# Attention and routed experts on one core: first expert rows loaded in a row, a router product in another bank, and written orders for TensorE and SyncE

## Chip, cores, metric

One core of a Trainium2 chip. The metric is the device time of one launch in microseconds (us); a change of under about 0.2% can't be told from none.

## What is computed

For each of 8 batches of 1856 rows: attention with squared ReLU, its output times u, and a two-level router (4 groups of 4 experts, the best group, then its best expert) in front of 16 experts of 256 x 1024 x 256. All is float32.

```python
scores = scale * np.matmul(z, z.transpose(0, 2, 1))
attn = np.maximum(scores, 0.0) ** 2
x = (u * np.matmul(attn, v)).reshape(B * S, D)
g_idx = np.argmax(x @ w_group, axis=1)          # g_w: its softmax
e_idx = np.argmax(xg @ w_expert[g], axis=1)     # e_w: its softmax
h = np.maximum(xg[mask_e] @ w1[g, e], 0.0)
out[tok_idx] = (g_w * e_w)[:, None] * (h @ w2[g, e])
```

## The kernel before

**Products in parts.** A float32 operand is split into a rounded high part and the rest, and a product is made of three passes (high by high, high by low, low by high). TensorE (PE) is busy with these nearly all the time.

**Attention** runs in 480 steps: 8 batches, 4 chunks of columns (512, 512, 512, 320), 15 blocks of keys each. `scores` runs some steps ahead of `attn_v`, which adds into the banks `o` (L409) with operands `al`, `ah` that VectorE (DVE) and ScalarE (ACT) make (L360, L361). At the end of a chunk `chunk_end` forms the chunk's rows `xT` (L431), splits them (`xh`, `xl`), and defers by step numbers: the router product `pl` (L486, L487, two pairs of products in a bank of `ps_m`), its copy `lgp` (ACT L494), a transposing load `lgx` on SyncE's queue (SP L497), and the transposed rows `rows` (SP L473).

**Routing.** The generator `route` is a chain of small DVE operations, a few at each step: it starts from `lgx` (L555), goes through the one-hot `oh` (L581) to the running counts `pre` (L602, L605), has two small PE products `pk` (L617 from `oh`, L618 from `pre`), and from these the places `di` (L630). GpSimd (POOL) then scatters the rows into `bucket` in HBM (L653). In the last batch chunks 2 and 3 are routed apart; they are named (7,2) and (7,3) here. The steps behind the last attention step are run by `early`, between the parts of the first two expert blocks.

**Experts 0 to 3** run as 12 blocks of up to 512 columns of the bucket (block 0 is 512 columns, 1: 512, 2: 384, 3: 320, 4: 256, 5: 368, 6: 512, 7: 256, 8: 336, 9: 304, 10: 256, 11: 512). Block i takes `xp_i` (a transposing load on SP, L790) and `meta_i` (L793) by `load_x`, `join_x` (DVE copy `xf`, L804; ACT `xh_m`, L809; DVE `xl_m`, L810), 48 products `ph` (L825 to L827) whose results go through `hh` (ACT L830) and `hl` (DVE L836), and 48 products `yT` (L910), copied to `yp` (ACT L913) and transposed back into `yr` on SP (L923) for the weighted scatter to the output. Blocks 0 and 1 use rows that were sorted earlier; block 2 and all later ones need every row scattered, those of (7,3) too (`more_rows` waits till `deferred` and `gens` are empty). The weights of experts 1 to 3 are loaded (`raw_e`, SP L184, L187) and split (L196, L197, L203, L204) inside an earlier block. Experts 4 to 15 follow with an order written for all engines, and are not touched.

**Order.** Within attention and blocks a scheduler orders each engine's instructions by its own model, except where `tc.manual_schedule` keeps the written order. Before, SP keeps it through the attention's end and blocks 0 and 1 (`queue`, closed at `i == NEARLY`, NEARLY = 2); PE, DVE, ACT and POOL are the scheduler's in all 12 blocks. Each engine and the SP queue run their instructions in their order: a waiting one holds all behind it.

Of the kernel before, what the change touches and what calls it, by code (L numbers as in the profile page):

```python
# [9 lines left out]
F32 = mybir.dt.float32  # L10
# [3 lines left out]
U16 = mybir.dt.uint16  # L14
# [5 lines left out]
P = 128  # L20
# [9 lines left out]
def tile_glu_attn_moe(  # L30
# [16 lines left out]
    ND = D // P  # L47
# [66 lines left out]
    def new_pl(name):  # L114
        return sb("pl", [P, 2048], U16, 2, name)
# [4 lines left out]
    def bank(pl, tag, name):  # L120
        return pl.tile([P, 512], F32, tag=tag, name=name)
# [94 lines left out]
    def new_w():  # L216
        return {"h": [], "l": [], "2": []}
# [203 lines left out]
    def chunk_end(s):  # L421
# [56 lines left out]
        pls = []  # L478

        def logits():  # L480
            ps = bank(ps_m, "m", f"pl_{b}_{c}")
            pls.append(ps)
            xh, xl = xhl
            held = pin if last else same
            for d in range(ND):
                held(nc.tensor.matmul(ps[0:LP, 0:w], whl[:, d, :], xh[:, d, 0:w], start=(d == 0), stop=False))  # L486
                nc.tensor.matmul(ps[0:LP, 0:w], wh0[:, d, :], xl[:, d, 0:w], start=False, stop=(d == ND - 1))  # L487
# [10 lines left out]
                lgx.rearrange("p t h l -> p (t h) l"), lgp[:, 0:nt].rearrange("p t h q -> p (t h q)")  # L498
            )

        LG = (7 if b == B - 1 and c < 2 else (9 if c == 2 else 8 if c == 0 else 7)) if s + 1 < NS - NK else 6 if last else 2
        XO = 2 if s + 1 < NS - NK else 0
        (split_x() if XO == 0 else defer(s + XO, split_x))
        (rest_x() if XO == 0 else defer(s + XO + 1, rest_x))
# [6 lines left out]
        defer(s + LG + (1 if XO else 0), logits_out)  # L511
        if not XO:
            defer(s + (7 if last else 5), to_rows)
        wait = 8 if last else (17 if c == 1 and b < B - 1 else 12 if c == 1 else 15) if s + 1 < NS - NK else 11
        alone = b == B - 1 and c >= NQ - 2
        if c % 2 or alone:
            gens.append((max(s + wait, PFILL[-1] + 2), route(b, c // 2, (c % 2,) if alone else (0, 1))))
# [8 lines left out]
    def run_gens(step, n):  # L526
        while gens and gens[0][0] <= step and n > 0:
            try:
                gap = next(gens[0][1])
                n -= 1  # L530
                if gap and step < 10 ** 9:
                    gens[0] = (step + gap, gens[0][1])
            except StopIteration:
                gens.pop(0)
# [251 lines left out]

    def load_x(name, r0, n):

        xp = new_pl(f"xp_{name}").rearrange("p (g q) -> p g q", g=4)
        nc.sync.dma_start_transpose(xp[:, :, 0:n], bucket16[ds(r0, n), 0:2 * D])  # L790
        meta = sb("meta", [P, 4, 2], I32, 7, f"meta_{name}")
        nt = (n + P - 1) // P
        nc.sync.dma_start(  # L793
            meta[:, 0:nt, :], bucket[ds(r0, nt * P), D:D + 2].rearrange("(t p) w -> p t w", p=P)
        )
        return xp, meta
# [239 lines left out]
    for s in range(NS):  # L1036
# [33 lines left out]
            prep_zm(nxt // NQ, nxt % NQ)  # L1070
        if s == NS - NK:
            load_rows(0)
        if s == NS - 9:
            load_rows(1)
        if s == NS - 8:
            xs.append(join_x(0, rows_b[0][0], blocks[0][2]))
# [16 lines left out]

    def early(i):
        run_deferred(late["at"])
        run_gens(late["at"], 4)
        late["at"] += 1
        more_rows(i)

# [322 lines left out]
    unsent = []  # L1422
    FILL = {1: (0, 1), 2: (2, 3), 7: (4, 5)}
    x = xs[0]
    for i, (e, r0, n) in enumerate(blocks):
        if i == NEARLY:
            queue.close()
        if i == 0:
            ld = 1
        else:  # L1430
            pe_ = blocks[i - 1][0]
            ld = pe_ + 2 if last_use[pe_] == i - 1 and pe_ + 2 < NOLD else None
        sp = []
        if ld is not None:
            wts[ld] = new_w()
            sp = [load_w(regs(ld)[0], wts[ld], pc, f"e{ld}") for pc in range(4)]

        def mid(f):
            if i < NEARLY:
# [27 lines left out]
        more_rows(i)  # L1467
        for j in FILL.get(i, ()):
            fill(j)
        if not last:  # L1470
            x = join_x(i + 1, rows_b[i + 1][0], blocks[i + 1][2])
        if i + 2 == NB:
# [17 lines left out]

        unsent = phase2_t(f"b{i}" if last else i, wts[e], hs, rows_b.pop(i)[1], n, next_view, mid2) or unsent

    duo_banks()
    in_order = ExitStack()
    written.append(True)
# [154 lines left out]
```

## Time and profile before

| | |
|---|---|
| median of 3 runs | 1420.11 us (1420.0 to 1420.81) |
| profiled execution | 1423.28 us, span 1421.5 us |
| TensorE, granted clock | busy 1409.7 us (99% of the span), clock 1.00 |
| DVE, ACT, POOL busy | 86%, 73%, 31% |
| blocks 0 to 11 | from 754 to 956 us of the span |

TensorE is the engine that sets the time, so what counts is where it pauses. A PE row of a timeline gives the start of a product and its modelled duration; products overlap, so the time between two starts is what one costs (about 0.23 us with 512 columns, 0.12 with 256). A pause is a longer step between two starts, and the brackets name what ended it.

### The profile page before, as it was taken

Reading aid. Unit: us, or ns where it says so; the run is one execution under the profiler, and the core shown is the slowest. Engines: PE = TensorE matmul, PEld = TensorE weight load, DVE = VectorE, ACT = ScalarE, POOL = GpSimd, SP = SyncE. Lnnn points to the kernel's source line nnn. Section 1 sums busy time; section 2 is a strip of 40 time slices with the busy share of each in tenths; the row PEclk is TensorE's granted clock in tenths of the full one; section 3 lists DMA queues with packets and bytes.
Section 4 is the critical chain, followed back from the end, with each engine's and each line's share of the span. In section 5 each row is a group of like instructions: output and inputs, shape, how many; then the busy total and the mean of one; then the engine's idle time right before and its main releaser. Section 6 shows DMA issues by size and latency. Waiting matters only on the chain.

```text
span 1421.5 us, 22629 instructions
## 1 busy us (share of the span) xinstructions
PE 1409.7 (99%) x6986; PEld 1216.5 (86%) x6986; DVE 1216.7 (86%) x2433; ACT 1042.2 (73%) x1836; POOL 435.1 (31%) x460
## 2 busy tenths in 40 slices
PE   9999999999999999999999999999999999999998
PEld 7888888888888888888788898988888888899997
DVE  7989999999989989999897578689777788888884
ACT  8877887787877878788775354357777777777773
POOL 0002012220222112201223232332445555555554
PEclk9999999999999999999999999999999999999999
DMA  6978979989899899897986476536565555566652
GB/s 235 250 189 228 243 167 257 237 203 226 188 254 228 191 240 211 225 239 165 244 207 159 126 206 146 118 84 145 141 146 131 147 142 136 141 152 151 154 140 59
DMA packets 402411, 257.78 MB, mean 181 GB/s; under 512 B 243827, under 2 KB 356238, under 8 KB 402288
## 3 DMA queue, kind: packets, MB, share of 16 engines
q1 hardware_dynamic: 390384, 225.29, 66.1%
q0 software_dynamic: 11824, 30.90, 7.9%
q8 instruction: 55, 0.90, 0.3%
q14 instruction: 68, 0.56, 0.1%
q10 hardware_dynamic: 80, 0.13, 0.0%
HBM read 110.65 MB, written 88.33 MB: 140 GB/s over the span
## 4 chain that ended last, share of the span: by engine, by line
PE 85%; DVE 6%; DMA 3%; issue 2%; ACT 2%; POOL 1%; SPq 1%; DVEq 0%; POOLq 0%; ACTq 0%
PE o L409 35%; PE duo_p L910 15%; PE duo_y L1372 6%; PE yT L910 4%; PE sc L371 4%; PE sc L372 4%; PE ph L825 2%; PE ph L826 2%; PE ph L827 2%; PE duo_w L1372 2%; PE duo_x L1372 2%; PE duo_p L1372 2%; PE duo_z L1372 2%; DMA out_dram<-y_w,meta_w 1%; PE pl L487 1%
## 5 line engine op out<-in xcount | busy, mean ns | idle before, releaser
L409 PE MATMUL o<-ah,vl 128*128 128x512 f32 (+1 forms) x960 | 354.5, 370 | 0.4 <-DVE ah L383 0.4
L409 PE MATMUL o<-ah,vh 128*128 128x512 f32 (+1 forms) x960 | 354.2, 369 | 0.0
L409 PE MATMUL o<-al,vh 128*128 128x512 f32 (+1 forms) x896 | 328.8, 369 | 0.2 <-DVE al L361 0.2
L653 POOL DMA_INDIRECT bucket<-rows,di x120 | 133.8, 1115 | 379.2 <-issue 220.1
L375 ACT ACTIVATE r<-sc 128x512 f32<-128x512 f32 (+1 forms) x300 | 172.5, 575 | 70.2 <-PE sc L372 49.8
L409 PEld LDWEIGHTS o<-ah,vl 128*128 128x128 f32 x960 | 180.2, 188 | 31.8 <-DVE ah L383 1.1
L409 PEld LDWEIGHTS o<-ah,vh 128*128 128x128 f32 x960 | 180.2, 188 | 30.0
L954 POOL DMA_INDIRECT out_dram<-y_w,meta_w x92 | 138.5, 1506 | 192.6 <-ACT y_w L948 145.3
L386 DVE TENSOR_TENSOR al<-r,ah 128x512 fp32r<-128x512 f32 (+1 forms) x268 | 181.0, 676 | 15.4 <-DVE ah L383 0.5
L409 PEld LDWEIGHTS o<-al,vh 128*128 128x128 f32 x896 | 167.9, 188 | 27.6 <-DVE al L386 0.4
L910 PE MATMUL duo_p<-hh_w,duo_w 128*128 128x496 f32 (+10 forms) x692 | 177.7, 371 | 0.0
L382 ACT ACTIVATE r<-r 128x512 f32<-128x512 f32 (+1 forms) x266 | 163.8, 616 | 8.5
L910 PEld LDWEIGHTS duo_p<-hh_w,duo_w 128*128 128x128 f32 x692 | 128.6, 188 | 16.7
L383 DVE CAST ah<-r 128x512 fp32r<-128x512 f32 (+1 forms) x266 | 109.8, 413 | 24.0 <-ACT r L382 20.3
L371 PE MATMUL sc<-zm,z2h 128*128 128x512 f32 (+1 forms) x300 | 116.6, 389 | 0.5 <-DVE zm L273 0.4
L372 PE MATMUL sc<-zm,z2l 128*128 128x512 f32 (+1 forms) x300 | 115.1, 384 | 0.0
L311 DVE STREAM_TRANSPOSE mt<-r 128x512 f32<-128x512 f32 x157 | 110.7, 705 | 0.7
L910 PE MATMUL duo_p<-hl_w,duo_w 128*128 128x496 f32 (+10 forms) x346 | 104.1, 371 | 0.0
L361 DVE TENSOR_TENSOR al<-at,ah 128x512 fp32r<-128x512 f32 (+1 forms) x180 | 101.3, 577 | 2.0 <-ACT ah L360 1.9
L360 ACT CAST ah<-at 128x512 fp32r<-128x512 f32 (+1 forms) x180 | 91.7, 530 | 7.6 <-DMA sym<-mt 5.0
L910 PE MATMUL yT<-hh,w_e 128*128 128x512 f32 (+6 forms) x352 | 74.1, 328 | 0.0
L954 POOL DMA_INDIRECT out_dram<-y,meta x33 | 39.6, 1199 | 106.4 <-DVE y L953 78.9
(263 smaller groups left out, 2879.6 us busy)
## 6 DMA issues: line engine op xcount, KB each, us to landing
sym<-mt SPq DMA_DIRECT2D x134, 256.0 KB
duo_r<-in_w_dram SPq DMA_DIRECT2D x48, 512.0 KB
at<-sym SPq DMA_DIRECT2D x88, 256.0 KB
bucket<-padrow SPq DMA_DIRECT2D x28, 528.0 KB
at<-sym SPq DMA_DIRECT2D x92, 160.0 KB
ut<-in_uT_dram SPq DMA_DIRECT2D x24, 512.0 KB
vr<-in_v_dram SPq DMA_DIRECT2D x23, 512.0 KB
raw_e<-in_w_dram SPq DMA_DIRECT2D x16, 512.0 KB
```

The costliest lines, as they stand in the source:

```text
L311: nc.vector.transpose(out=t2.rearrange("p (j t x) -> p t j x", t=KT, x=32), in_=a.rearrange("p (t j x) -> p t j x", t=KT, x=32))
L371: held(nc.tensor.matmul(ps[:, 0:w], z2h[:, ks], zm, start=True, stop=False))
L372: held(nc.tensor.matmul(ps[:, 0:w], z2l[:, ks], zm, start=False, stop=True))
L375: held(nc.scalar.activation(out=a, in_=ps[:, 0:w], func=AF.Relu, scale=1.0 / S))
L382: held(nc.scalar.activation(out=a, in_=a, func=AF.Square))
L383: held(nc.vector.tensor_copy(out=ah, in_=a))
L386: held(nc.vector.tensor_sub(out=al, in0=a, in1=f32(ah)))
L409: held(nc.tensor.matmul(oa[d][:, 0:QW[b][c]], (vh if q else vl)[:, d0:d0 + P], al if q == 2 else ah, start=(i == 0 and q == 0), stop=end a ...
L653: nc.gpsimd.indirect_dma_start(out=views[(b * NQ + 2 * half + hs[h]) * NT + i], out_offset=bass.IndirectOffsetOnAxis(ap=di[0:n, i0 + i:i0 ...
L910: nc.tensor.matmul(o, wt["2"][f // 2][:, w0:w0 + P], hs[f][q // 2][:, c0:c0 + n], start=(at == 0), stop=(at == 3 * NF - 1))
L954: nc.gpsimd.indirect_dma_start(out=outs(), out_offset=bass.IndirectOffsetOnAxis(ap=meta[0:m, t, 1:2], axis=0), in_=y[0:m], in_offset=None, ...
L1372: nc.tensor.matmul(out, a, b, start=(q == 0 and m in (1, 5)), stop=(q == 2), skip_group_check=True)
```

## The change

1. `load_x`: the rows of block 0 (`xp_0`) go into a buffer of the tag `ut` (2 buffers) rather than of the tag of `new_pl`; and `load_rows(1)` runs 5 steps earlier, one step behind `load_rows(0)`.
2. The last router product, that of (7,3), goes into a bank of `ps_s` (used by scores and `ph`) rather than of `ps_m`, one step earlier (LG 5 for 6); its routing starts one step earlier (wait 7 for 8), and each `early` runs 5 steps of a generator for 4.
3. PE runs blocks 0 and 1 in the written order too (`region`).
4. SP keeps the written order through all 12 blocks (`queue.close()` stands behind the loop), and the next expert's weights are asked for one block earlier (`needs`, `ask`, `asked`).

```diff
--- before.py
+++ after.py
@@ -478,7 +478,7 @@
         pls = []
 
         def logits():
-            ps = bank(ps_m, "m", f"pl_{b}_{c}")
+            ps = bank(*((ps_s, "s") if last else (ps_m, "m")), f"pl_{b}_{c}")
             pls.append(ps)
             xh, xl = xhl
             held = pin if last else same
@@ -498,7 +498,7 @@
                 lgx.rearrange("p t h l -> p (t h) l"), lgp[:, 0:nt].rearrange("p t h q -> p (t h q)")
             )
 
-        LG = (7 if b == B - 1 and c < 2 else (9 if c == 2 else 8 if c == 0 else 7)) if s + 1 < NS - NK else 6 if last else 2
+        LG = (7 if b == B - 1 and c < 2 else (9 if c == 2 else 8 if c == 0 else 7)) if s + 1 < NS - NK else 5 if last else 2
         XO = 2 if s + 1 < NS - NK else 0
         (split_x() if XO == 0 else defer(s + XO, split_x))
         (rest_x() if XO == 0 else defer(s + XO + 1, rest_x))
@@ -511,7 +511,7 @@
         defer(s + LG + (1 if XO else 0), logits_out)
         if not XO:
             defer(s + (7 if last else 5), to_rows)
-        wait = 8 if last else (17 if c == 1 and b < B - 1 else 12 if c == 1 else 15) if s + 1 < NS - NK else 11
+        wait = 7 if last else (17 if c == 1 and b < B - 1 else 12 if c == 1 else 15) if s + 1 < NS - NK else 11
         alone = b == B - 1 and c >= NQ - 2
         if c % 2 or alone:
             gens.append((max(s + wait, PFILL[-1] + 2), route(b, c // 2, (c % 2,) if alone else (0, 1))))
@@ -786,7 +786,11 @@
 
     def load_x(name, r0, n):
 
-        xp = new_pl(f"xp_{name}").rearrange("p (g q) -> p g q", g=4)
+        if name == 0:
+            xp = sb("ut", [P, ND, 512], F32, 2, f"xp_{name}").rearrange("p c q -> p (c q)").bitcast(U16)
+        else:
+            xp = new_pl(f"xp_{name}")
+        xp = xp.rearrange("p (g q) -> p g q", g=4)
         nc.sync.dma_start_transpose(xp[:, :, 0:n], bucket16[ds(r0, n), 0:2 * D])
         meta = sb("meta", [P, 4, 2], I32, 7, f"meta_{name}")
         nt = (n + P - 1) // P
@@ -1070,7 +1074,7 @@
             prep_zm(nxt // NQ, nxt % NQ)
         if s == NS - NK:
             load_rows(0)
-        if s == NS - 9:
+        if s == NS - NK + 1:
             load_rows(1)
         if s == NS - 8:
             xs.append(join_x(0, rows_b[0][0], blocks[0][2]))
@@ -1093,7 +1097,7 @@
 
     def early(i):
         run_deferred(late["at"])
-        run_gens(late["at"], 4)
+        run_gens(late["at"], 5)
         late["at"] += 1
         more_rows(i)
 
@@ -1422,18 +1426,28 @@
     unsent = []
     FILL = {1: (0, 1), 2: (2, 3), 7: (4, 5)}
     x = xs[0]
+    asked = {}
+
+    def needs(i):
+        pe_ = blocks[i - 1][0]
+        return pe_ + 2 if last_use[pe_] == i - 1 and pe_ + 2 < NOLD else None
+
+    def ask(ld):
+        wts[ld] = new_w()
+        return [load_w(regs(ld)[0], wts[ld], pc, f"e{ld}") for pc in range(4)]
+
     for i, (e, r0, n) in enumerate(blocks):
+        if i == 0:
+            region.enter_context(tc.manual_schedule(engines={mybir.EngineType.PE}))
         if i == NEARLY:
-            queue.close()
+            region.close()
         if i == 0:
             ld = 1
         else:
-            pe_ = blocks[i - 1][0]
-            ld = pe_ + 2 if last_use[pe_] == i - 1 and pe_ + 2 < NOLD else None
-        sp = []
-        if ld is not None:
-            wts[ld] = new_w()
-            sp = [load_w(regs(ld)[0], wts[ld], pc, f"e{ld}") for pc in range(4)]
+            ld = needs(i)
+        sp = asked.pop(ld, [])
+        if ld is not None and not sp:
+            sp = ask(ld)
 
         def mid(f):
             if i < NEARLY:
@@ -1467,6 +1481,8 @@
         more_rows(i)
         for j in FILL.get(i, ()):
             fill(j)
+        if 0 < i < NB - 1 and needs(i + 1) is not None:
+            asked[needs(i + 1)] = ask(needs(i + 1))
         if not last:
             x = join_x(i + 1, rows_b[i + 1][0], blocks[i + 1][2])
         if i + 2 == NB:
@@ -1490,6 +1506,7 @@
 
         unsent = phase2_t(f"b{i}" if last else i, wts[e], hs, rows_b.pop(i)[1], n, next_view, mid2) or unsent
 
+    queue.close()
     duo_banks()
     in_order = ExitStack()
     written.append(True)
```

The two texts have other line numbers behind L789: what is L790, L793, L804, L825, L836, L910, L923 before is L794, L797, L808, L829, L840, L914, L927 in the changed kernel.

SyncE's order at the end of attention, before. `xp_0`, `xp_1` are the rows of blocks 0 and 1, `lgx_7_2` is the router product of (7,2), transposed; the loads of `eli` and `rli` fetch the addresses for `xp_1`:

```order
L790 DMA_TRANSPOSE xp_0_9547<-bucket_69 128x4x512
L793 ISA
L793 DMA meta_0_9549<-bucket_69 128x4x2
L497 DMA_TRANSPOSE lgx_7_2_9534<-lgp_7_2_9533 128x8x48
L473 DMA_TRANSPOSE rows_7_2_9530<-pl_7_2_9532 128x4x128 x4
L773 TENSOR_LOAD eli_108
L773 ISA x2
L774 TENSOR_LOAD rli_109
L774 ISA x2
L790 ISA
L790 DMA_TRANSPOSE xp_1_9658<-bucket_69 128x4x512
```

The same place in the changed kernel:

```order
L794 DMA_TRANSPOSE xp_0_9547<-bucket_69 128x4x512
L797 ISA
L797 DMA meta_0_9549<-bucket_69 128x4x2
L773 TENSOR_LOAD eli_108
L773 ISA x2
L774 TENSOR_LOAD rli_109
L774 ISA x2
L794 ISA
L794 DMA_TRANSPOSE xp_1_9583<-bucket_69 128x4x512
L797 ISA
L797 DMA meta_1_9585<-bucket_69 128x4x2
L497 DMA_TRANSPOSE lgx_7_2_9534<-lgp_7_2_9533 128x8x48
```

`xp_1`, its addresses and its `meta` have moved from behind the rows of (7,2) to ahead of `lgx_7_2`.

TensorE's order around the small product `pk` of (7,2), in block 0, before (`ph_0_5` is the sixth of block 0's eight `ph`, of six products each; 33 products of `ph` stand ahead of the first `pk`, 39 of the second):

```order
L825 MATMUL ph_0_5_9882<-xh_m0_9682,w1l_e0_0_9468 128x512
L826 MATMUL ph_0_5_9882<-xh_m0_9682,w1h_e0_9467 128x512
L827 MATMUL ph_0_5_9882<-xl_m0_9683,w1h_e0_9467 128x512
L617 LDWEIGHTS tri_75
L617 MATMUL pk_7_1_0_9841<-oh16_7_1_0_9753,tri_75 128x64
L825 MATMUL ph_0_5_9882<-xh_m0_9682,w1l_e0_1_9509 128x512
```

The same product in the changed kernel:

```order
L830 MATMUL ph_0_2_9832<-xh_m0_9682,w1h_e0_9467 128x512
L831 MATMUL ph_0_2_9832<-xl_m0_9683,w1h_e0_9467 128x512
L617 LDWEIGHTS tri_75
L617 MATMUL pk_7_1_0_9843<-oh16_7_1_0_9753,tri_75 128x64
L618 LDWEIGHTS ones_73
L618 MATMUL pk_7_1_0_9843<-pre_7_1_0_9757,ones_73 128x64
L829 MATMUL ph_0_3_9846<-xh_m0_9682,w1l_e0_0_9468 128x512
```

Both products of `pk` now stand behind 18 products of `ph` (the third is `ph_0_2`). That of (7,3), which stood in block 1 (ahead of its 22nd and its 37th `ph` product), now stands in the middle of block 0's `yT`, behind 48 `ph`, the four products of `pl` (7,3), which stand behind `ph_0_4`, and 24 `yT`.

SyncE's order ahead of block 8, before (`yr_4` is block 4's result on its way back):

```order
L790 DMA_TRANSPOSE xp_7_11184<-bucket_69 128x4x256
L923 DMA_TRANSPOSE yr_4_10810<-yp_4_10809 128x4x128 x2
L790 ISA
L790 DMA_TRANSPOSE xp_8_11379<-bucket_69 128x4x336
L184 ISA
L184 DMA raw_e3_0_11073<-in_w1_dram 128x1024
```

In the changed kernel:

```order
L794 DMA_TRANSPOSE xp_7_11186<-bucket_69 128x4x256
L797 ISA
L797 DMA meta_7_11188<-bucket_69 128x2x2
L927 DMA_TRANSPOSE yr_6_11199<-yp_6_11198 128x4x128 x4
L794 ISA
L794 DMA_TRANSPOSE xp_8_11381<-bucket_69 128x4x336
```

`xp_8` has moved from behind `yr_4` to behind the four transposes of `yr_6`, which wait for block 6's end.

## Rows read from the trace of the kernel before

**Rows 1.** Part 1 of the page: busy us, share of the span, instructions.
```profile
PE 1409.7 (99%) x6986; PEld 1216.5 (86%) x6986; DVE 1216.7 (86%) x2433; ACT 1042.2 (73%) x1836; POOL 435.1 (31%) x460
```
**Rows 2.** PE's waits over the span: us in total, times, longest.
```profile
PE ph L825 <- ACT xh_m L809: 2.5, 3, 1.8
```
**Rows 3.** Windows: busy us of each engine, granted clock, DMA share.
```profile
780.00:820.00 40.00, 38.24 (x195) 34.06 (x195) 24.65 (x62) 14.20 (x24) 9.56 (x10) 1.00 0.51 139
```
**Rows 4.** PE timeline at the starts of blocks 1, 2, 5, 9: start, duration.
```profile
776.84 0.39 PE L910 MATMUL yT<-hl,w_e 128*128 128x512 f32 x1
777.40 0.50 PE L825 MATMUL ph<-xh_m,w1l_e 128*128 128x512 f32 x1 [0.17 <-issue]
...
799.39 0.39 PE L910 MATMUL yT<-hl,w_e 128*128 128x512 f32 x1
801.54 0.44 PE L825 MATMUL ph<-xh_m,w1l_e 128*128 128x384 f32 x1 [1.76 <-ACT xh_m L809]
...
844.03 0.28 PE L910 MATMUL yT<-hl,w_e 128*128 128x256 f32 x1
844.82 0.44 PE L825 MATMUL ph<-xh_m,w1l_e 128*128 128x368 f32 x1 [0.51 <-ACT xh_m L809]
...
908.79 0.32 PE L910 MATMUL yT<-hl,w_e 128*128 128x336 f32 x1
909.35 0.41 PE L825 MATMUL ph<-xh_m,w1l_e 128*128 128x304 f32 x1 [0.24 <-ACT xh_m L809]
```
**Rows 5.** POOL timeline: the last scatter of (7,3).
```profile
792.87 1.02 POOL L653 DMA_INDIRECT bucket<-rows,di  x1 [0.30 <-issue]
```
**Rows 6.** SP timeline, 738 to 800 us: start and time of the issue.
```profile
742.93 4.30 SPq L790 DMA_TRANSPOSE xp<-bucket  x1
...
751.75 1.19 SPq L497 DMA_TRANSPOSE lgx<-lgp  x1
752.98 5.55 SPq L473 DMA_TRANSPOSE rows<-pl  x4
760.14 1.96 SPq L790 DMA_TRANSPOSE xp<-bucket  x1
...
795.89 1.42 SPq L790 DMA_TRANSPOSE xp<-bucket  x1
```
**Rows 7.** DVE timeline at the start of block 2.
```profile
799.59 1.03 DVE L804 COPY xf<-xp 128x1536 uint16<-128x1536 uint16 x1 [3.29 <-DMA xp<-bucket]
```
**Rows 8.** DVE timeline, 742 to 776 us: xT, xf_0, the route of (7,2).
```profile
743.77 1.29 DVE L431 TENSOR_TENSOR xT<-o,ut 128x512 f32<-128x512 f32 x2
...
749.85 1.36 DVE L804 COPY xf<-xp 128x2048 uint16<-128x2048 uint16 x1
...
754.31 0.35 DVE L555 COPY lgf<-lgx 128x320 uint16<-128x320 uint16 x1
...
759.49 0.16 DVE L605 TENSOR_TENSOR pre<-pre,oh 128x16 bf16<-128x16 bf16 x1
```
**Rows 9.** PE timeline in block 0: first product, pk, the four pl.
```profile
754.39 0.39 PE L825 MATMUL ph<-xh_m,w1l_e 128*128 128x512 f32 x1
...
761.90 0.20 PE L617 MATMUL pk<-oh,tri 128*128 128x64 bf16 x1
...
769.21 0.31 PE L486 MATMUL pl<-xh,whl 128*48 128x320 f32 x1
...
769.78 0.39 PE L910 MATMUL yT<-hh,w_e 128*128 128x512 f32 x1
```
**Rows 10.** PE timeline: the start of block 7, and the end of its yT.
```profile
882.71 0.28 PE L825 MATMUL ph<-xh_m,w1l_e 128*128 128x256 f32 x1
...
895.14 0.32 PE L825 MATMUL ph<-xh_m,w1l_e 128*128 128x336 f32 x1
```
**Rows 11.** SP timeline: the four transposes of yr_6.
```profile
883.95 5.13 SPq L923 DMA_TRANSPOSE yr<-yp  x4
```
**Rows 12.** DVE timeline ahead of block 9.
```profile
907.69 0.87 DVE L804 COPY xf<-xp 128x1216 uint16<-128x1216 uint16 x1
```

## The prediction

> **What bounds the kernel.** The page's first part comes first: TensorE (PE) is busy 1409.7 of 1421.5 us [rows 1], so a gain can only come from PE's pauses. The list of PE's waits shows what is left of them: under experts 0 to 3, three waits for `xh_m`, 2.5 us together, one of 1.8 [rows 2]. The windows show the granted clock at 1.00 around the longest, so a pause there costs its own length and no clock after it [rows 3]. The timeline at the block borders then gives each pause as the step between two starts, less one ordinary step [rows 4]:
> - block 1: 777.40 - 776.84 - 0.23 = 0.33 us, and 0.1 more in its first step;
> - block 2: 801.54 - 799.39 - 0.23 = **1.92**;
> - block 5: 844.82 - 844.03 - 0.12 = **0.67**, and 0.1 more in its first step;
> - block 9: 909.35 - 908.79 - 0.15 = 0.41.
>
> That is 3.5 us, 0.25% of the time: all that this change could win where it acts. About 0.2% (2.8 us) is what a measurement of this kernel can tell from no change.
>
> **Where the pauses come from.** Block 2's rows can be loaded only when the last scatter has landed. That scatter starts at 792.87 [rows 5], the load follows at 795.89 [rows 6], the copy of its result starts at 799.59 [rows 7], and PE goes on at 801.54: 5.65 us from load to product. The scatters are late because the routing is: `xp_1` is issued at 760.14, behind the rows of (7,2) [rows 6], and the scatters stand behind it; and `pk` of (7,3) stands in block 1.
>
> **The change, part by part.** Everything up to 745 us is as it was, and so is everything behind block 11.
>
> *Block 2's pause goes (-1.92).* By the order, `pk` of (7,3) stands in block 0's `yT`, near 773 us (below) instead of in block 1, so the scatters end some 10 us sooner. `xp_2` then waits only for the four transposes of `yr_0` ahead of it on SP. Those of `yr_6` take 5.13 us [rows 11]; if `yr_0` starts as late as 785, `xp_2` is issued at 790 and PE could start at 796, ahead of 800. So nothing of the 1.92 stays; bounds 1.0 and 1.92.
>
> *Block 1's pause goes (-0.44).* `xp_1` is in place some 10 us sooner and `xf_1` stands inside the route of (7,3), about a microsecond sooner than it was. Bounds 0 and 0.44.
>
> *Block 5's pause goes (-0.77).* It ends a chain of late weights of expert 2, which are now asked for a block earlier. Bounds 0.5 and 0.77.
>
> *Block 9's pause, half of it (-0.2).* Its `xf` starts at 907.69 [rows 12], late behind other DVE work, not behind SP. The order moves little there. Bounds 0 and 0.41.
>
> *A new wait at `pk` of (7,2) (+1.9).* In a written order PE stops at `pk` if `pre` isn't ready, with 30 ready products behind it. When does PE come there? The 33 products ahead of the first `pk` took 761.90 - 754.39 = 7.51 us, 0.2276 each [rows 9]; behind 18 it comes at 754.39 + 18 x 0.2276 = 758.5. When is `pre` ready? DVE's chain from `lgf` (754.31) to the last `pre` (759.65) took 5.34 us [rows 8]; by DVE's order it now has two `hl` within it instead of one, 0.6 more: 760.25, and 0.15 to the product. So 760.4 - 758.5 = 1.9. Bounds: 1.0, where the order inside the chain saves what the second `hl` costs and a little more; and 4.1, where `lgx` starts later (next).
>
> *Two loads ahead of `lgx` (7,2) on SP (0).* Before, `lgx` starts at 751.75, as soon as its source is copied [rows 6]. Now `xp_1` (1.96 us), its `meta` and its addresses stand ahead, and `xp_0` must wait for the second `xT` product, which ends at 745.06 [rows 8], since `xp_0` took a buffer of the tag of `ut`. `xp_0` took 4.30 us from 742.93 [rows 6] because the queue ahead of it was full till about 747; that fullness doesn't wait for `xT`. If so, `xp_0` is out at 747.2 as before, and `xp_1` by 750.8: `lgx` isn't held. If the 4.30 count from 745.06, `xp_0` is out at 749.4, 2.1 later, and with 1.6 for the addresses (the time from the end of the four `rows` at 758.53 to `xp_1` at 760.14) `lgx` starts near 754, 2.25 late: the 4.1 above. I take the first; the second is a rival.
>
> The same fork decides `xf_0`. It starts 749.85 - 742.93 = 6.9 us behind the start of `xp_0`'s issue [rows 6, 8]; counted from 745.06 that is 752.0, 2.1 late, and the `al` behind it on DVE would hold PE. [...]
>
> *A second new wait, at `pk` of (7,3) (+0.6).* PE comes there behind 72 products and four of `pl`, which took 769.78 - 769.21 = 0.57 together [rows 9]: 754.39 + 16.4 + 0.57 = 771.35, plus the first wait 1.9: 773.25. The chain of (7,3) is paced by PE itself, since the last `hl` stands in it behind the last `ph` (near 769.1); the rest, some 20 small operations and `xf_1` within (1.36 by `xf_0`'s row [rows 8]), takes 4.7 by their rows before: 773.8. Bounds 0 and 2.3; the upper counts the 11.7 us that went from `pl` to `pre` before, with the weight splits that the order now puts behind it.
>
> *SP's written order in blocks 7 to 11 (+0.4).* `xp_8` stands behind `yr_6`. Block 7's products end at 895.14 less six of block 8 at 0.157: 894.2 [rows 10]. `yr_6` starts at 883.95 and takes 5.13 [rows 11], and 5.65 from load to product gives 894.7: 0.5 late; block 8 is smaller than block 2 (336 columns for 384), so 0.3. Bounds 0 and 1.2, if DVE is busy with other work when the rows land. `xp_11` stands behind three transposes of `yr_9` in a block of 256 columns: 0.1, bounds 0 and 0.6. The other blocks have a microsecond or more of room.
>
> **Sum:** -1.92 - 0.44 - 0.77 - 0.2 + 1.9 + 0.6 + 0.4 = -0.4 us, so 1422.9 against the profiled execution's 1423.28 us. That execution lies 3.2 us above the median of 1420.11; carried to the median: **1419.7 us**. One wait is exchanged for another: the routing's pause in front of block 2 becomes a pause in block 0.
>
> **Rivals.**
> - *The waits go and none comes* (1417.1): the chain of (7,2) keeps up with PE, and both `pk` find their operands within 0.5 us. For it: DVE's chain has gaps, and the scheduler has moved the small operations up. Against: 5.34 us from `lgf` to `pre`, with PE at `pk` 4.2 us behind `lgf`. It gives -3.5 (all pauses gone) + 0.5 = -3.0.
> - *SP's written order makes late what PE waits for* (1423.3): `xp_0` and `xp_1` hold `lgx` by 2.25 us, and in blocks 8 and 11 the row loads stand behind `yr` at the upper bounds. 4.1 + 0.6 + 1.2 + 0.6 - 3.3 = +3.2. It decides from the point where the wait at the first `pk` passes 4 us. For it: `xp_0` must now wait till 745.06. Against: SP's queue was full until about then.
> - *The change does nothing that shows*: if block 2 still waits for something else (the four transposes of `yr_0` ahead of `xp_2` on SP, say) and the new waits are half as long, the sum is within half a microsecond of zero as well; that time can't be told from my forecast, and is counted with it.
>
> **How the numbers follow.** My forecast with its neighbours 0.64, the first rival 0.2, the second 0.16. The range goes from the first rival, 1417.0, to the second, 1423.5; beyond it I leave 0.08 on either side. Faster by over 0.2% (under 1417.3) is most of the first rival, 0.2; slower by over 0.2% (over 1422.9) most of the second, 0.16; the rest 0.64.
>
> **What would show it.** Right: PE's list of waits names `pk` (L617 or L618) with DVE's `oh` or `pre`, some 2 us in block 0 and under 1 in its `yT`; no pause at block 2's first product; the scatters start about 755 and the last ends before 785; `xp_2` lands over 5 us before block 2. Wrong: `pk` shows no wait (first rival); `lgx` (7,2) starts at 753 or later, or blocks 8 and 11 start over 1 us late (second); or the pause at block 2 is still there.

## The result, and the profile after

The changed kernel takes 1428.22 us (median of 6 runs, 1427.22 to 1432.15), the kernel before 1420.07 (6 runs, 1419.39 to 1420.81): ratio 1.0062, 95% interval 1.0052 to 1.0073 (the two medians alone give 1.0057). It is **slower by 8.15 us**. I had forecast 1419.7 (1417.0 to 1423.5), "no change" as the likeliest. The prediction was wrong, and the time lies outside its range.

The profiled execution took 1431.18 us, span 1429.5. Part 1 of its page, as in [rows 1]:

```profile
PE 1412.9 (99%) x6986; PEld 1220.3 (85%) x6986; DVE 1220.2 (85%) x2433; ACT 1047.5 (73%) x1836; POOL 436.5 (31%) x460
```

The same 6986 products are there, PE is busy 3.2 us longer, and the span is 8.0 longer. So most of it is pauses, and something made products themselves slower. PE's waits of after, which answer to [rows 2] (us in total, times, longest):

```profile
PE ph L829 <- ACT xh_m L813: 3.9, 2, 2.1
PE pk L618 <- DVE pre L605: 2.4, 2, 1.8
...
PE yT L914 <- DVE hl L840: 0.5, 1, 0.5
```

The two `pk` waits are those I forecast. The two waits for `xh_m`, 2 us each, and the one for `hl` are not. The timeline of PE says where they are: start and duration, at the `pk` of (7,2), that of (7,3), inside `yT` of block 8, and at the first products of blocks 9 and 11.

```profile
756.32 0.39 PE L831 MATMUL ph<-xl_m,w1h_e 128*128 128x512 f32 x1
757.14 0.20 PE L617 MATMUL pk<-oh,tri 128*128 128x64 bf16 x1 [0.44 <-DVE oh L581]
759.14 0.21 PE L618 MATMUL pk<-pre,ones 128*128 128x64 bf16 x1 [1.80 <-DVE pre L605]
759.17 0.77 PE L829 MATMUL ph<-xh_m,w1l_e 128*128 128x512 f32 x1
...
774.51 0.19 PE L618 MATMUL pk<-pre,ones 128*128 128x64 bf16 x1 [0.60 <-DVE pre L605]
...
907.14 0.84 PE L914 MATMUL yT<-hl,w_e 128*128 128x336 f32 x2 [0.46 <-DVE hl L840]
...
909.35 0.32 PE L914 MATMUL yT<-hl,w_e 128*128 128x336 f32 x1
911.43 0.41 PE L829 MATMUL ph<-xh_m,w1l_e 128*128 128x304 f32 x1 [1.77 <-ACT xh_m L813]
...
937.60 0.40 PE L914 MATMUL yT<-hl,w_e 128*128 128x256 f32 x2
940.11 0.80 PE L829 MATMUL ph<-xh_m,w1l_e 128*128 128x512 f32 x1 [2.11 <-ACT xh_m L813]
940.70 0.63 PE L830 MATMUL ph<-xh_m,w1h_e 128*128 128x512 f32 x1
941.13 0.63 PE L829 MATMUL ph<-xh_m,w1l_e 128*128 128x512 f32 x1
```

The last two rows show the second surprise: these starts are 0.43 apart, where a product with 512 columns takes 0.23 elsewhere. Windows of after around those places, with the columns of [rows 3] (PE's busy time first, the granted clock third from the end):

```profile
756.00:761.00 5.00, 2.77 (x10) 1.85 (x9) 4.14 (x20) 2.90 (x8) 3.80 (x4) 0.82 0.88 216
761.00:766.00 5.00, 5.00 (x22) 4.01 (x20) 2.71 (x5) 3.13 (x6) 4.08 (x5) 0.84 1.02 375
...
911.00:916.00 5.00, 4.57 (x22) 4.57 (x23) 3.65 (x12) 1.62 (x5) 1.90 (x2) 0.68 0.36 83
...
940.00:945.00 5.00, 4.89 (x15) 3.93 (x15) 3.59 (x7) 0.06 (x1) 1.99 (x2) 0.66 0.76 149
945.00:950.00 5.00, 5.00 (x23) 4.13 (x22) 2.97 (x5) 2.95 (x6) 0.89 (x1) 1.00 0.17 42
```

The granted clock fell behind three of the pauses: in windows of 1 us it stands at 0.50 from 760 to 762, from 913 to 916 and from 941 to 943, and at 1.00 again from 763, 917 and 944 on. PE ran some us of products at half the clock there, 0.43 us for one with 512 columns.

**The account of the two profiled executions**, each pause a step between two starts less an ordinary one:

| place | before | after |
|---|---|---|
| blocks 1, 2, 5 [rows 4] | 0.43, 1.92, 0.77 | none |
| `pk` (7,2) in block 0 | – | 2.55 (0.6 + 1.96), and 1.7 of products at the lower clock |
| `pk` (7,3) in block 0 | – | 0.8 |
| block 8 starts; its `yT` | – | 0.4; 0.99 |
| block 9 starts | 0.41 | 1.93, and 1.5 at the lower clock |
| block 11 starts | – | 2.27, and 1.7 at the lower clock |
| sum | 3.5 | 13.8 |

That is +10.3. Against it, this execution of after was 1.95 us ahead before anything moves: the first `pl` product of 512 columns stands at 744.43 for 746.38. (Block 0's first product stands 2.25 earlier, 752.14 for 754.39 [rows 9], since two products of attention now come behind it.) Together +8.35, and the spans differ by 8.0; the 0.35 between them is not placed.

### The profile page after: what moved, and what is told of

Read it like the earlier page. It is cut to its first block, busy times and chain, and to the rows that moved or that the text cites. A ratio compares the mean times of both kernels' runs of the same rounds, so it can differ in the third digit from the quotient of the medians.

```text
span 1429.5 us, 22637 instructions
## 1 busy us (share of the span) xinstructions
PE 1412.9 (99%) x6986; PEld 1220.3 (85%) x6986; DVE 1220.2 (85%) x2433; ACT 1047.5 (73%) x1836; POOL 436.5 (31%) x460
## 4 chain that ended last, share of the span: by engine, by line
PE 89%; issue 3%; DVE 3%; DMA 2%; POOL 1%; ACT 1%; SPq 0%; POOLq 0%; DVEq 0%; ACTq 0%
PE o L409 39%; PE duo_p L914 14%; PE duo_y L1376 6%; PE sc L371 5%; PE sc L372 5%; PE yT L914 4%; PE ph L829 2%; PE ph L830 2%; PE ph L831 2%; PE duo_x L1376 2%; PE duo_w L1376 2%; PE duo_p L1376 2%; PE duo_z L1376 2%; DMA out_dram<-y_w,meta_w 1%; PE pl L487 1%
## 5 line engine op out<-in xcount | busy, mean ns | idle before, releaser
L653 POOL DMA_INDIRECT bucket<-rows,di x120 | 137.3, 1144 | 378.3 <-issue 217.8
L914 PE MATMUL duo_p<-hh_w,duo_w 128*128 128x496 f32 (+10 forms) x692 | 177.9, 371 | 0.0
L914 PEld LDWEIGHTS duo_p<-hh_w,duo_w 128*128 128x128 f32 x692 | 128.6, 188 | 16.6
L914 PE MATMUL duo_p<-hl_w,duo_w 128*128 128x496 f32 (+10 forms) x346 | 104.0, 371 | 0.0
L840 DVE SCALAR_TENSOR_TENSOR hl<-ph,hh 128x512 fp32r<-128x512 f32 (+6 forms) x96 | 50.9, 546 | 34.7 <-ACT hh L834 34.3
L834 ACT ACTIVATE hh<-ph 128x512 fp32r<-128x512 f32 (+6 forms) x96 | 45.6, 487 | 45.5 <-PE ph L831 44.6
```

Of the source, the lines that this page charges most:

```text
L653: nc.gpsimd.indirect_dma_start(out=views[(b * NQ + 2 * half + hs[h]) * NT + i], out_offset=bass.IndirectOffsetOnAxis(ap=di[0:n, i0 + i:i0 ...
L914: nc.tensor.matmul(o, wt["2"][f // 2][:, w0:w0 + P], hs[f][q // 2][:, c0:c0 + n], start=(at == 0), stop=(at == 3 * NF - 1))
```

## The experiments

In all of them items 1 and 2 of the change stay, and the weights are asked for a block early, unless the edit says otherwise. "Before" was run beside each; its medians were 1420.02, 1419.55 and 1420.02 us in the three sets.

### Each written order undone alone, both undone, and item 1 alone

**SP's written order ends at block 2 again** (all edits are against the changed kernel):

```diff
         if i == NEARLY:
             region.close()
+            queue.close()
...
-    queue.close()
     duo_banks()
```

> The changed kernel with one edit undone: SyncE keeps the written order through blocks 0 and 1 only, as before; the rest of the change stays. Theory: of the 9.6 us that the changed kernel loses against before from the last chunk on, 8.9 us lie in blocks 8, 9 and 11 (pauses of 0.4, 1.0, 2.0 and 2.4 us and 3 us of products at the lower clock behind them), and they come from SyncE's order. Without it block 9 has its old pause of 0.5 back and the rest is gone: 1428.2 - 8.9 + 0.5 = 1419.8 us, the pauses at the two pk stay (2.6 and 0.8 us, and 1.7 at the lower clock). Rival: the pauses in blocks 9 and 11 come from something that PE's order in blocks 0 and 1 has shifted: then 1426 to 1428.

Measured: 1423.65 us (1421.79 to 1426.59), ratio 1.0022 (1.0013 to 1.0032). All pauses in blocks 8 to 11 are gone, so SP's order made every one of them. What is left is larger than the 1419.8 expected, and it is `pk`. The profiled execution, the slowest of the nine and 2.9 us above their median, shows it: SP's issue, DVE's copy of what it loads, and the two `pk` products of (7,3).

```profile
764.17 1.20 SPq L497 DMA_TRANSPOSE lgx<-lgp  x1
...
771.19 0.39 DVE L555 COPY lgf<-lgx 128x320 uint16<-128x320 uint16 x1 [3.08 <-DMA lgx<-lgp]
...
774.42 0.20 PE L617 MATMUL pk<-oh,tri 128*128 128x64 bf16 x1 [1.59 <-DVE oh L593]
776.24 0.21 PE L618 MATMUL pk<-pre,ones 128*128 128x64 bf16 x1 [1.61 <-DVE pre L605]
```

From the issue of `lgx` of (7,3) to its use are 7.0 us, and PE stood 1.75 + 1.77 us at that `pk`, with 2.7 lost at the lower clock behind it (0.52 granted from 777 to 782). In after the same load was issued at 765.21 and used at 769.47, 4.3 us, with 0.8 at `pk`. The 2 MB of expert 1's weights stand ahead of it in both.

**PE's order in blocks 0 and 1 left to the scheduler**:

```diff
-        if i == 0:
-            region.enter_context(tc.manual_schedule(engines={mybir.EngineType.PE}))
-        if i == NEARLY:
-            region.close()
```

> The changed kernel with one edit undone: PE's order in blocks 0 and 1 is the scheduler's again; SyncE's written order through all 12 blocks stays. Theory: the waits at the two pk go (2.6 and 0.8 us), and with them the 1.7 us at the lower clock: 1428.2 - 5.1 = 1423.1 us; the pauses in blocks 8, 9 and 11 stay. Rival: the scheduler's order only moves the wait, since the routing's chain is as long: 1426 to 1428, with a wait of 2 us for pre at another place.

Measured: 1424.51 us (1423.6 to 1426.01), ratio 1.0031 (1.0019 to 1.0043); expected 1423.1. `pk` waits nowhere; block 9 pauses 1.92 us, with 1.5 at the lower clock from 907.7 us on, and block 11 2.27, with 1.6. Its waits for `xh_m` are those of after (4.0 us in total, longest 2.1). The clock behind block 9, whose first product is at 906.56:

```profile
909.00:912.00 3.00, 3.00 (x17) 3.00 (x16) 1.27 (x5) 1.11 (x3) 1.94 (x2) 0.65 0.65 153
```

**Both undone**, the two edits together:

> The changed kernel with both orders undone (PE's in blocks 0 and 1, SyncE's behind block 1); what stays is the early loads of blocks 0 and 1, the router product in the score bank one step earlier, and the weights asked for a block earlier. Theory: the pauses in front of blocks 1, 2 and 5 are gone (3.2 us) and no wait takes their place: 1420.1 - 3.2 = 1416.9 us, no drop of the clock. Rival: pk is reached early by the scheduler's order too (it stands in block 0 for both chunks) and waits 2 us there: 1419 to 1420.

Measured: 1417.8 us (1417.0 to 1419.62), ratio 0.9985 (0.9976 to 0.9994); expected 1416.9. No block waits. The window that answers to [rows 3]:

```profile
780.00:820.00 40.00, 40.00 (x216) 37.08 (x215) 25.75 (x55) 15.33 (x28) 10.67 (x12) 1.00 0.71 176
```

PE is busy all of it, where it was 38.24 of 40. So the earlier loads, routing and weights win about 2.2 us in medians, and the two written orders give it back and more. I had counted 3.3 for the same pauses. I read them from an execution 3.2 us above the median, of which 1.95 lie ahead of block 0; so the median execution of before paused some 1.2 us less in the blocks (an estimate from these two numbers). In medians: PE's order costs 1423.65 - 1417.8 = 5.9 without SP's and 1428.22 - 1424.51 = 3.7 with it; SP's costs 6.7 without PE's and 4.6 with it. They overlap: 12.6 one by one, 10.4 together.

**Item 1 alone**, as an edit of the kernel before:

```diff
-        xp = new_pl(f"xp_{name}").rearrange("p (g q) -> p g q", g=4)
+        if name == 0:
+            xp = sb("ut", [P, ND, 512], F32, 2, f"xp_{name}").rearrange("p c q -> p (c q)").bitcast(U16)
+        else:
+            xp = new_pl(f"xp_{name}")
+        xp = xp.rearrange("p (g q) -> p g q", g=4)
...
-        if s == NS - 9:
+        if s == NS - NK + 1:
             load_rows(1)
```

> Before with one edit of the change alone: the rows of block 0 in a buffer of ut, and load_rows(1) behind load_rows(0). Theory: the scatters of chunks 0 to 2 of the last batch start some 10 us earlier, but block 2 waits for the last three scatters, whose pk still stands in block 1: block 2's pause shrinks by under 1 us, 1419.3 to 1420.3. Rival: the early rows alone take block 2's pause away: 1418.0. Other rival, the prediction's: the transposing load lgx of (7,2) is held by the two row loads and PE waits for it: 1421 to 1422.

Measured: 1420.4 us (1419.36 to 1420.68), ratio 1.0003 (0.9994 to 1.0012), no difference, and about the upper end of what was expected. Block 2's pause went by this alone, which I had not expected, but block 1 now pauses 1.6 us for the 0.33 of [rows 4], and block 5 keeps its 0.69:

```profile
776.90 0.50 PE L829 MATMUL ph<-xh_m,w1l_e 128*128 128x512 f32 x1 [1.46 <-ACT xh_m L813]
```

The rows lay ready: `xf_1` (774.44) stands on DVE behind `lgf` of (7,3), which waited till 773.35 for its `lgx`, 3.4 us behind the issue, where before it was 2.7. Why that load took longer was not followed up.

### The wait at `pk`

**`pk` two parts later**, SP's order undone as well:

```diff
-        yield {(B - 1, 0, 0): 5, (B - 1, 1, 0): 5, (B - 1, 1, 1): 1, (B - 2, 1, 0): 5}.get((b, half, hs[0]), 9 if half or b == B - 1 else 7)
+        yield {(B - 1, 0, 0): 5, (B - 1, 1, 0): 7, (B - 1, 1, 1): 2, (B - 2, 1, 0): 5}.get((b, half, hs[0]), 9 if half or b == B - 1 else 7)
```

> The kernel of e1_sp_two_blocks (PE written in blocks 0 and 1, SyncE written in these two alone) with pk of (7,2) 12 products later in block 0 (behind the four pl) and pk of (7,3) some 36 products later, in block 1. Theory: the waits in e1 (2.7 us at the first pk, 3.5 at the second, 2.5 at the lower clock) come from the place of pk alone; here both operands are ready some 1 us before PE comes, and the last scatter still lands before block 2: 1423.7 less some 6 = 1417.5 to 1418.5 us, no wait for pk. Rival: a written order costs by itself (the scheduler's order had the weights' parts in turn): over 1420 with pauses elsewhere in blocks 0 and 1.

Measured: 1419.34 us, but from 1417.44 to 1424.05 in eleven runs; ratio 1.0006 (0.9996 to 1.0016). The profiled execution took 1417.44 and has no wait at `pk`. Most of what the order cost is gone in the best executions; in others it is back. No trace of a long one was taken, so what waits there is open; the varying load of the next experiment fits.

**Two of expert 1's four weight loads (`w2`) behind `lgx` of (7,3)**, SP's order undone:

```diff
-        return [load_w(regs(ld)[0], wts[ld], pc, f"e{ld}") for pc in range(4)]
+        return [load_w(regs(ld)[0], wts[ld], pc, f"e{ld}") for pc in range(2 if ld == 1 else 4)]
...
+            if ld == 1 and f == 5:
+                sp.extend(load_w(regs(1)[0], wts[1], pc, "e1") for pc in (2, 3))
```

> The kernel of e1_sp_two_blocks with two of the four weight loads of expert 1 (1 MB of 2) issued behind lgx of (7,3) on SyncE's queue instead of ahead of it. Theory: in e1 lgx of (7,3) took 7.0 us from its issue to its use (4.2 in the changed kernel), behind the weights and the scatters; here it takes under 4, and the wait at the second pk shrinks from 3.5 to under 1: 1421 to 1422 us against 1423.7. Rival: the scatters alone hold lgx, or the chain on VectorE does: no change, 1423 to 1424.

Measured: 1421.21 us (1420.04 to 1422.31), as expected, 2.4 below the same kernel with all weights ahead. `lgx` was issued at 763.43 and used at 767.23, 3.8 us, and the wait at the `pk` of (7,3) is 0.6 in this execution:

```profile
772.51 0.19 PE L618 MATMUL pk<-pre,ones 128*128 128x64 bf16 x1 [0.42 <-DVE pre L605]
```

The 3.5 us of the trace with all weights ahead are those of its slowest execution, and another with the same orders in these blocks waited 1.77 (next section); so the conclusion rests on the medians. The first `pk` keeps 2.24 us: the chain of DVE operations (5.34 us in [rows 8]) is longer than 18 products (4.1), and `lgx` of (7,2) is late too (its source is copied at 749.40, and it goes out at 750.14).

### Where SP's order hurts: blocks 8 to 11

What these blocks wait for is read from three timelines of after. SP:

```profile
892.61 3.77 SPq L983 DMA_DIRECT2D bucket<-padrow  x2
896.49 4.28 SPq L927 DMA_TRANSPOSE yr<-yp  x2
...
931.16 2.01 SPq L794 DMA_TRANSPOSE xp<-bucket  x1
```

DVE:

```profile
903.90 1.23 DVE L1174 TENSOR_TENSOR ov_big<-ov_le,ov_it 128x1024 f32<-128x1024 f32 x1 [4.02 <-DMA yr<-yp]
905.05 0.50 DVE L840 SCALAR_TENSOR_TENSOR hl<-ph,hh 128x336 fp32r<-128x336 f32 x1
...
909.82 0.83 DVE L808 COPY xf<-xp 128x1216 uint16<-128x1216 uint16 x1
...
936.62 1.34 DVE L808 COPY xf<-xp 128x2048 uint16<-128x2048 uint16 x1
```

And ACT at the end of block 10:

```profile
938.04 1.07 ACT L917 COPY yp<-yT 128x512 uint16<-128x512 uint16 x2 [4.86 <-issue]
939.00 1.06 ACT L813 CAST xh_m<-xf 128x1024 fp32r<-128x1024 f32 x1
```

The same places before, SP, DVE, then ACT:

```profile
871.67 1.36 SPq L979 DMA_DIRECT2D bucket<-padrow  x2
...
896.13 3.92 SPq L923 DMA_TRANSPOSE yr<-yp  x2
...
908.59 1.97 SPq L790 DMA_TRANSPOSE xp<-bucket  x1
```
```profile
901.36 1.23 DVE L1170 TENSOR_TENSOR ov_big<-ov_le,ov_it 128x1024 f32<-128x1024 f32 x1 [2.27 <-DMA yr<-yp]
```
```profile
931.49 1.05 ACT L809 CAST xh_m<-xf 128x1024 fp32r<-128x1024 f32 x1 [2.46 <-DVE xf L804]
...
936.24 1.07 ACT L913 COPY yp<-yT 128x512 uint16<-128x512 uint16 x2 [3.69 <-PE yT L910]
```

*Blocks 8 and 9.* An operation of DVE (`ov_big`, which shares its buffer with the results of block 7) waits till those have been read out by `yr_7`. The written order puts two padding writes (`padrow`) right ahead of `yr_7`; before, they had gone out 24 us ahead of it (871.67 and 896.13). `yr_7` lands 2.5 us later (903.90 for 901.36), and behind the waiting `ov_big` (nothing starts on DVE from 899.9 to 903.90) stand the last `hl` of block 8 and `xf_9`, which starts 2.1 later than in [rows 12].

*Block 11.* Before, `xp_11` went out at 908.59, ahead of block 9's `yr`. In the written order it stands behind `yr_9`: 931.16, 22.6 later. `xf_11` ends at 937.96, and ACT takes `xh_m` behind two copies of block 10's result (938.04), where the scheduler had it ahead of them. So of the 2.27 about 1.0 is ACT's changed place and the rest the late load. That the scheduler moved ACT because the load was late is inferred.

**SP's order ends at block 10**, all else as in the change:

```diff
+        if i == 10:
+            queue.close()
...
-    queue.close()
```

> The changed kernel with SyncE's written order ended ahead of block 10 instead of behind block 11. Theory: block 11's pause (2.3 us, and 1.7 at the lower clock) goes, since the scheduler then loads xp_11 early and ScalarE's xh_m of block 11 stands ahead of the copies of block 10's results; blocks 8 and 9 keep theirs: 1428.2 - 4.0 = 1424.2 us. Rival: block 11 is late for the routing of what is loaded behind it (the rows of the next experts on the same queue): 1428, with the pause still there.

Measured: 1427.15 us (1427.03 to 1428.2), ratio 1.0053 (1.0039 to 1.0066): a miss, 1424.2 was expected. Block 11's pause is gone, but other pauses took its place, 0.76 at block 10 and 1.30 within its `yT`. PE at the second `pk` of (7,3), and at these two places:

```profile
774.01 0.19 PE L618 MATMUL pk<-pre,ones 128*128 128x64 bf16 x1 [1.61 <-DVE pre L605]
...
926.16 0.39 PE L829 MATMUL ph<-xh_m,w1l_e 128*128 128x256 f32 x1 [0.59 <-ACT xh_m L813]
...
937.39 0.50 PE L914 MATMUL yT<-hl,w_e 128*128 128x256 f32 x2 [1.14 <-DVE hl L840]
```

SP and DVE show where the two come from. `xp_11` now goes out right behind `xp_10` (919.99 behind 917.84), and `xp_10` takes 6.9 us from issue to use, where it took 4.9 in after. And DVE takes `xf_11` ahead of the last four `hl` of block 10, which stood ahead of it in after:

```profile
924.70 0.76 DVE L808 COPY xf<-xp 128x1024 uint16<-128x1024 uint16 x1 [4.39 <-DMA xp<-bucket]
...
935.10 1.33 DVE L808 COPY xf<-xp 128x2048 uint16<-128x2048 uint16 x1
...
936.93 1.40 DVE L840 SCALAR_TENSOR_TENSOR hl<-ph,hh 128x256 fp32r<-128x256 f32 x4
```

Block 0 differs from after as well, though the orders there are the same. PE waited 2.5 us at the first `pk`, and the clock did not fall behind it. So PE came sooner to the `pk` of (7,3) and waited 1.77 there, where after has 0.8, and the clock fell behind that wait (0.57 granted from 775 to 779).

**The same with PE left to the scheduler**:

> The kernel of e2_pe_scheduled with SyncE's written order ended ahead of block 10. The same edit won only 1.1 us on the changed kernel, with pauses of 0.8 in front of block 10 and 1.3 within its yT in place of block 11's. Theory: block 11's pause and the low clock behind it go (4.0 us), the two new pauses in block 10 come (2.1): 1424.5 - 1.9 = 1422.6 us, clock at 1.00 from block 10 on. Rival: block 10's two pauses were this one execution's, and all of it is won: 1420.5.

Measured: 1422.75 us (1421.16 to 1423.68), ratio 1.0017 (1.0008 to 1.0026), as expected. The pauses at block 10 are 0.84 and 1.30, and that of block 11 is gone. Block 9's 1.92 is there, with no fall of the clock behind it.

**The padding writes one block later**, PE left to the scheduler, SP's order whole:

```diff
-    FILL = {1: (0, 1), 2: (2, 3), 7: (4, 5)}
+    FILL = {1: (0, 1), 2: (2, 3), 8: (4, 5)}
```

> The kernel of e2_pe_scheduled (SyncE written through all 12 blocks) with the two writes of padding rows to the bucket for experts 4 and 5 issued one block later (FILL 8 for 7), so that on SyncE's queue they stand behind the transposes of yr_7 and the load of xp_9 instead of ahead of them. Theory: VectorE's ov_big2 waits for yr_7 to have left its buffer, and holds the hl of block 8 and xf_9 behind it; with the padding out of the way yr_7 lands some 2 us sooner, the pause within block 8's yT (0.5 us) goes and block 9's shrinks from 1.9 to under 0.5: 1424.5 - 2.0 = 1422.5 us. Rival: yr_7 and xp_9 are late because they stand behind xp_8 and yr_6, not for the padding: no change, 1424 to 1425.

Measured: 1421.8 us (1421.29 to 1423.23), ratio 1.0012 (1.0003 to 1.0021): 2.7 below the run with PE left to the scheduler, as expected. SP and PE:

```profile
889.89 3.32 SPq L927 DMA_TRANSPOSE yr<-yp  x2
...
898.36 3.76 SPq L983 DMA_DIRECT2D bucket<-padrow  x2
```
```profile
904.40 0.41 PE L829 MATMUL ph<-xh_m,w1l_e 128*128 128x304 f32 x1 [0.46 <-ACT xh_m L813]
...
931.78 0.50 PE L829 MATMUL ph<-xh_m,w1l_e 128*128 128x512 f32 x1 [2.11 <-ACT xh_m L813]
```

With `yr_7` ahead of the padding again, block 8's `yT` doesn't pause and block 9's pause is 0.63 for 1.92 (under 0.5 was expected, and before has 0.41). So the padding's place on SP made the first of these and most of the second. Block 11's 2.27 stays, as it should; the clock fell behind none of them in this execution.

### What a pause costs beyond its length

**Pauses of chosen places**: `xh_m` of four blocks is copied several times over on ACT, in the kernel with both orders undone.

```diff
-        nc.scalar.copy(out=xh[:, :, 0:n], in_=xf[:, :, 0:n])
+        for _ in range({3: 14, 4: 16, 6: 11, 10: 18}.get(name, 1)):
+            nc.scalar.copy(out=xh[:, :, 0:n], in_=xf[:, :, 0:n])
```

> The kernel of e3_both_undone with ScalarE's copy xh_m repeated, with the same result, 14 times ahead of block 3, 16 ahead of block 4, 11 ahead of block 6 and 18 ahead of block 10, so that PE pauses there by about 1, 2, 3 and 4 us. Theory: the granted clock stays at 1.00 behind pauses under 2 us and falls behind those over 2.2 us, and each fall costs another 1.5 to 2 us of products at the lower clock. Rival: the clock falls for what stands around blocks 0, 9 and 11 (load, transfers), not for the pause: then no fall here, or one behind every pause.

Measured: 1457.69 us in one run. The pauses came out longer than meant, 6.2, 7.4, 10.6 and 6.0 us, and behind each PE ran 3.7 to 5.4 us at the lower clock (0.51 granted from 820.0 to 824.7, behind the first), which cost 1.8 to 2.8. A second kernel with {3: 7, 4: 8, 6: 4, 10: 15}:

> The kernel of e7_pauses with fewer repeated copies: 7 ahead of block 3, 8 ahead of block 4, 4 ahead of block 6 and 15 ahead of block 10, for pauses of about 1, 2, 3 and 4 us. In e7 the pauses were 6 to 10.6 us, and behind each the products ran at the lower clock for 4 to 6 us, 1.8 to 2.8 us lost. Theory: no fall behind 1 us; a fall behind 3 and 4, with some 2 us lost behind each; 2 us lies near the border, where both were seen. Rival: the loss grows with the pause in proportion: 0.3 us behind 1, 0.6 behind 2, 1 behind 3.

Measured: 1432.99 us in one run, with pauses of 2.17, 3.11 and 4.03 us (none at block 3). Windows behind the first two, columns as above:

```profile
832.00:835.00 3.00, 3.00 (x18) 3.00 (x17) 1.66 (x5) 0.77 (x2) 2.39 (x3) 0.56 0.88 102
...
862.50:865.50 3.00, 3.00 (x8) 2.38 (x9) 2.96 (x6) 0.00 (x0) 0.11 (x1) 0.53 0.83 207
```

Behind the third 0.56 was granted in the 3.5 us from 930.5. Each fall cost 1.4 to 1.5 us. So a fall costs nearly the same behind 2 and behind 4 us, not in proportion to the pause. Over all traces, pauses of about 2 us went either way:

| pause | a fall behind it | no fall |
|---|---|---|
| 1.77 at the `pk` of (7,3) | SP's order ended at block 10 | – |
| 1.92 or 1.93 at block 9 | after; PE left to the scheduler | both runs with SP's order ended at block 10 |
| 1.92 at block 2 | – | before [rows 3, 4] |
| 2.17 at block 4 | the added copies | – |
| 2.27 at block 11 | after; PE left to the scheduler | the padding moved |
| 2.2 to 2.7, in two parts, at the first `pk` | after | SP's order ended at block 2 (two kernels), or at block 10 |

The theory of the first of these two experiments (none under 2 us, a fall above 2.2) does not hold. With PE left to the scheduler, blocks 8 and 9 pause alike (0.6 and 1.92) whether SP's order is whole or ended at block 10, and the clock fell in the first trace and not in the second. So the length alone doesn't settle it between these, and I draw no bound. Behind all pauses of 3 us and more there was a fall.

### Both undone, and the weights too

The two edits of "both undone" and the weight loads behind `lgx`:

> The kernel of e3_both_undone (both orders undone, 1417.8 us) with two of the four weight loads of expert 1 issued behind lgx of (7,3), as in e8. Theory: no pause is left there for PE to lose, so the median stays within 0.5 us of e3's, with fewer slow executions: 1417.3 to 1418. Rival: the later weights are late themselves for block 1's second half: a pause of 1 us or more within yT of block 1, 1419 or more.

Measured: 1417.85 us (1416.93 to 1418.69), ratio 0.9981 (0.9972 to 0.9990). With its twin (1417.8) it beats both kernels: 10.4 us below the change, and 2.2 below the kernel before, at the limit of what can be told.

## Why the prediction was wrong, and where it was right

**Right.**
- *The pauses of blocks 1, 2 and 5* went, and the chain moved as forecast: the last scatter starts at 779.55 for 792.87 [rows 5], and `xp_2` goes out at 786.98. That block 2 needs the `pk` in block 0 for it is not shown: with item 1 alone its pause went too, behind a block 1 that started 1.6 late. The forecast of "as late as 785" for `yr_0`'s start erred on the safe side: it started at 781.31.
- *The waits at `pk`* came where the order put them: 2.55 us for 1.9 at (7,2), 0.8 for 0.6 at (7,3). The second agreement is luck. The 1.7 us at the lower clock behind the first `pk` made PE come that much later to the second; without them, in the run with SP's order ended at block 10, the wait was 1.77.
- *`lgx` of (7,2)*, in part. `xp_0` was issued when `xT` had ended, in 2.15 us for 4.30 [rows 6], and so was out as early as forecast. But `lgx` was held, against "isn't held": its source was copied at 749.33, and it went out 1.04 us later, behind `xp_1` and its `meta`. That is 1.0 of the second rival's 2.25. DVE stood 0.63 us for it, about what the first wait has over its 1.9. The other half of that fork, `xf_0`, was not late: it started at 747.90, 4.76 us behind its issue, which is the 749.85 of [rows 8] less the lead of 1.95; PE waited 0.52 us for an `al` behind it, 0.19 before. The DVE and SP rows of `lgx`:

```profile
748.33 1.00 ACT L494 COPY lgp<-pl 48x1024 uint16<-48x1024 uint16 x1
...
750.37 1.21 SPq L497 DMA_TRANSPOSE lgx<-lgp  x1
...
752.99 0.35 DVE L555 COPY lgf<-lgx 128x320 uint16<-128x320 uint16 x1 [0.63 <-DMA lgx<-lgp]
```

- *Block 8* starts 0.4 late for 0.3.

**Wrong, in order of size.**
1. *"... so a pause there costs its own length and no clock after it"* [rows 3]. This was read from one window behind one pause of 1.92 us, and carried to a pause forecast at 1.9 and to sums of up to 4.1. The clock fell three times in the profiled execution, 4.9 us together. The spread of the runs goes with it: the mean granted clock was 0.996 in the two longest (1431.18, 1432.15) and 0.997 or 0.998 in the four others, and 0.002 of 1429 us is 2.9 us, most of the 3.9 between them.
2. *"`xp_11` stands behind three transposes of `yr_9` in a block of 256 columns: 0.1, bounds 0 and 0.6."* Block 11's pause measured 2.27. I counted the time on SP and not that, with the late load, the scheduler puts ACT's `xh_m` behind the copies of block 10's result. That is about 1.0 of it; the rest is a load 22.6 us later than before, of which I had only three transposes' worth.
3. *"Its `xf` starts ... late behind other DVE work, not behind SP. The order moves little there"* (-0.2). Block 9 got 1.5 worse and block 8's `yT` 0.99 besides. The DVE work ahead of `xf_9` waited for a buffer, and that for a transfer on SP: an `<-DMA yr<-yp` of 2.27 us stood in the trace of before, at 901.36, one step further back than I looked.
4. *"The chain of (7,3) is paced by PE itself"* (+0.6, at most 2.3). It hangs on a load: `lgx`, with 2 MB of weights ahead of it, was used at 769.47 in after, and at 769.00 where it had gone out 1.8 us sooner (SP's order ended at block 10). The wait was 1.77 there, and 3.5 in the slowest execution with SP's order undone, over the bound.

The *second rival* (SP's written order makes late what PE waits for, 1423.3) was the right mechanism at blocks 8 to 11, and at `lgx` for less than half of its price; it had 0.16 and too small a price, since its bounds counted the SP times alone. Without the falls of the clock and items 2 and 3, what is left of the account is 2.55 + 0.8 + 0.4 + 0.41 - 3.5 = +0.7 us, where the forecast had -0.4; most of that difference is the first `pk`.

## What to carry to other kernels

A written order on one queue must be read for everything that it moves, not only for what it was written for: list what now stands ahead of each load and each write-back, then follow each write-back to the buffer it frees and the engine that waits there. Leaving an engine to the scheduler is no constant either: the order of one engine changes what the scheduler does with the others. And before a pause is traded for another of about 2 us on TensorE, price the products behind it at the lower clock as well: 1.4 to 1.7 us each time that the clock fell behind a pause of 1.9 to 2.6 us here. Read the pauses, too, from an execution near the median.

## What was not expected of the hardware

- Behind a pause of 2.17 us PE went on at full clock for about 1 us (0.12 us a product of 256 columns from 830.37 to 831.2) and only then fell (0.21 a product, 0.56 granted in the 3 us from 832); behind block 9's 1.92, with PE left to the scheduler, it was the same (first product at 906.56, low from 907.7). Behind 3.1 us it was low at once (0.43 a product of 512 columns, 0.53 granted in the 3 us from 862.5). Of four traces with 1.92 or 1.93 us at block 9 two show a fall. Pauses of 6 to 10.6 us cost no more than 2.8 us of slow products on top of their length.
- A transposing load of the same small tile (`lgx` of (7,3), one issue of 1.2 to 1.5 us) took 4.3, 5.6 and 7.0 us from issue to use with 2 MB of weights ahead of it on SP's queue, and 3.8 with half of them. In two of these kernels it was issued 1.8 us apart (763.42 and 765.21) and used 0.5 apart (769.00 and 769.47): an earlier issue won little.
